# Attention and two expert layers on one core: the loads of the raw weights go from SyncE's queue to GpSimd's

## The chip, the core and the metric

The kernel runs on one core of one Trainium2 chip. The core has TensorE (PE in the rows, its weight loads PEld), VectorE (DVE), ScalarE (ACT), GpSimd (POOL) and SyncE (SP), and 16 DMA engines that every queue of the core feeds. The metric is the device time of one execution in microseconds, of which the median over some runs is given.

## The reference

```
kv  = einsum('bhsd,bhse->bhde', k, v)          # 8 batches, 8 heads, 576 tokens, 64 wide
out = einsum('bhsd,bhde->bhse', q, kv)
out = out / sqrt(mean(out * out, -1) + 1e-06) * g_norm
x   = out.transpose(0, 2, 1, 3).reshape(4608, 512)
h = x @ w_in1;  x = (h * clip(h + 3, 0, 6) / 6) @ w_out1      # 512 -> 2048 -> 512
h = x @ w_in2;  x = (h * cos(h)) @ w_out2
```

The four weight matrices arrive as 64-bit words, the rest as float32.

## The kernel before

The 4608 tokens are nine superblocks of 512. Each layer takes its 2048 inner features as eight pairs of 128-row blocks. A weight matrix comes in eight pieces of 1 MB (one pair each): `ri` is a piece of a w_in, `ro` of a w_out. The function `raw_load` (L208) loads a piece into one of three buffers with the tag `raw`; these buffers serve other tiles too. `decode` makes float32 of the 64-bit words: ScalarE at L245, VectorE at L247, L251 and L254, ScalarE again at L258 (a sum of squares), after which the raw buffer is free. The float32 piece is called `di` or `do`.

The program starts with attention for superblock 0: `kv_load` (L383, L388) and the loads of the last rows of k and v (`tail`, L933) bring k and v of the four pairs of heads of batch 0, `kv_pair` multiplies them on TensorE (L403), VectorE copies the result into `kvbd` (L412), `q_load` (L429) brings q, and `chunk` turns each 128 tokens of q into x: transpose (L435), copy on ScalarE (L446), product (L455), squares and copy on ScalarE (L459, L460), a short chain on VectorE (L465 to L475), transpose (L481), scale into `xr` (L487). Then superblock 0 goes through layer 1 in float32: `plain_1` (L1016, the product with `di`; L1022 and L1023 make `u` of it) and `plain_2` (L1031, the product with `do`), for 16 row blocks f, while the weights are also split into float16 halves. All later superblocks, and all of layer 2, run as Strassen-like products in float16 (L841, L660, L713).

All DMAs before the change are issued by SyncE, one after the other, in the order that a list scheduler gives the instructions of each engine when the program is built. An engine takes its instructions strictly in that order: one that waits holds all behind it.

Of the kernel before, what the change touches and what calls it, by code (L numbers as in the profile page):

```python
# [16 lines left out]
TOP = 2.0 ** 12  # L17
# [2 lines left out]
TWO_PI = 6.283185307179586  # L20
REBIAS = 2.0 ** -((1023 - 127) // 8)

# Winograd's form of Strassen's product, C = A B in 2x2 blocks:
#   S1 = A21+A22  S2 = S1-A11  S3 = A11-A21  S4 = A12-S2
#   T1 = B12-B11  T3 = B22-B12  T2 = T3+B11  N4 = B21-T2
# products in the order issued, with the accumulator each goes to:
PRODS = (
    ("A11", "B11", "P"),
    ("A12", "B21", "Q"),
# [26 lines left out]
def attention_moe_kernel(  # L56
# [12 lines left out]
    nc = tc.nc  # L69
    B, H, S, D = q.shape  # L70
# [4 lines left out]
    P = 128  # L75
# [39 lines left out]
    c3_t, gn, gs = (col() for _ in range(3))  # L115
    kvbd = const.tile([P, 2, NP, P], F32, name="kvbd")

    # ---- stages: each generator emits one stage per turn, so that consecutive
    # ---- stages, which wait on each other across engines, lie a turn apart
    active = []  # L120

    def start(gen):
# [22 lines left out]
        turn_of[0] += 1  # L145
        return ps_m.tile([P, 512], F32, tag=tag, name=name, bufs=2 if tag == "t" else 1)

    # ---- scales
    def pow2_scale(mx, name, squares, res, at=None):
        """[P, 1] magnitudes, or sums of squares that bound theirs -> res = (s, 1/s), s a power  # L150
        of two with s * max in [TOP, 2 TOP)."""
        pt = ps_scratch(f"pt_{name}")
        nc.tensor.transpose(out=pt[0:1, 0:P], in_=mx, identity=ident)
        m1 = col(p=1)
        nc.vector.tensor_reduce(
            out=m1, in_=pt[0:1, 0:P], axis=AX.X, op=ALU.max, apply_absolute_value=True
        )
        yield
        pb = ps_scratch(f"pb_{name}")
        nc.tensor.matmul(out=pb[:, 0:1], lhsT=ones_row, rhs=m1, start=True, stop=True)  # L160
        t = sm_p.tile([P, 1], F32, tag="sc", name=f"t_{name}")
        lo, hi = (2.0 ** -96, 2.0 ** 96) if squares else (2.0 ** -48, 2.0 ** 48)
        nc.vector.tensor_scalar(out=t, in0=pb[:, 0:1], scalar1=hi, scalar2=lo, op0=ALU.min, op1=ALU.max)
        pw = sm_p.tile([P, 1], U32, tag="pw", name=f"pw_{name}")
        if squares:
            nc.vector.tensor_scalar(
                out=pw, in0=t.bitcast(U32), scalar1=1, scalar2=0x3F800000,
                op0=ALU.logical_shift_right, op1=ALU.bitwise_and,
            )
        else:  # L170
            nc.vector.tensor_scalar(
                out=pw, in0=t.bitcast(U32), scalar1=0x7F800000, scalar2=None, op0=ALU.bitwise_and
            )
        s, inv = at or (col(), col())
        nc.vector.tensor_scalar(out=inv, in0=pw.bitcast(F32), scalar1=(2.0 ** 63 if squares else 1.0) / TOP, scalar2=None, op0=ALU.mult)
        nc.vector.reciprocal(out=s, in_=inv)
        res[name] = (s, inv)
        yield
# [12 lines left out]
    fac = [col(NG) for _ in range(2)]  # L191
    least = {}
    u0, b0, c0 = (col(NG) for _ in range(3))
    scale = {}
    scaled = set()
    sc1 = {}
    sc2 = {}

    # ---- weights: float64 words -> float32 -> scaled f16 hi and lo
    def raw_load(layer, kind, i):  # L200
        r = raw_p.tile([P, 1024, 2], U32, tag="raw", name=f"r{kind}{layer}_{i}")
        if kind == "i":
            src = w_ins[layer][:, 4 * i * P:4 * (i + 1) * P].rearrange("(k p) c -> p k c", p=P)
            dst = r.rearrange("p (k f) two -> p k (f two)", k=KD)
        else:
            src = w_outs[layer][2 * i * P:2 * (i + 1) * P, :].rearrange("(a p) c -> p a c", p=P)
            dst = r.rearrange("p (a e) two -> p a (e two)", a=2)
        nc.sync.dma_start(out=dst, in_=src)  # L208
        return r

    def group_scale(layer, kind, gi):
        """The scale of the weights of pairs 2 gi and 2 gi + 1."""
        mx = col()
        nc.vector.tensor_reduce(out=mx, in_=m_w[kind, layer][:, 2 * gi:2 * gi + 2], axis=AX.X, op=ALU.max)
        yield
        s, inv = s_w[kind, layer]
        yield from pow2_scale(
            mx, f"{kind}{layer}_{gi}", True, scale, (s[:, gi:gi + 1], inv[:, gi:gi + 1])
        )
        scaled.add((kind, layer, gi))  # L220

    def group_factors(layer):
        """fac = what brings each group's products to the scale common to all."""
        ts, tt = nc.vector.tensor_scalar, nc.vector.tensor_tensor
        fs = []
        for kind in "io":
            s, inv = s_w[kind, layer]
            m, f = col(), col(NG)
            nc.vector.tensor_reduce(out=m, in_=inv, axis=AX.X, op=ALU.max)
            yield  # L230
            ts(out=f, in0=s, scalar1=m, scalar2=None, op0=ALU.mult)
            yield
            nc.vector.reciprocal(out=f, in_=f)
            least[kind, layer] = m
            fs.append(f)
        yield
        tt(out=fac[layer], in0=fs[0], in1=fs[1], op=ALU.mult)
        yield

    def decode(r, t, sq):  # L240
        """float64 words r -> float32 t; sq = the sum of their squares. The upper half of a
        float64, taken for a float32, has the upper bits of the exponent for its exponent: a
        factor brings the bias to float32's, and what lies below its range to nothing."""
        hi, lo, tu = r[:, :, 1], r[:, :, 0], t.bitcast(U32)
        nc.scalar.activation(out=t, in_=hi.bitcast(F32), func=AF.Abs, scale=REBIAS)  # L245
        yield
        nc.vector.tensor_scalar(  # L247
            out=tu, in0=tu, scalar1=3, scalar2=0x7FFFFFFF, op0=ALU.logical_shift_left, op1=ALU.bitwise_and
        )
        yield  # L250
        nc.vector.scalar_tensor_tensor(  # L251
            out=tu, in0=hi, scalar=0x80000000, in1=tu, op0=ALU.bitwise_and, op1=ALU.bitwise_or
        )
        nc.vector.scalar_tensor_tensor(  # L254
            out=tu, in0=lo, scalar=29, in1=tu, op0=ALU.logical_shift_right, op1=ALU.bitwise_or
        )
        yield
        nc.scalar.activation(out=r[:, 0:512].bitcast(F32), in_=t, func=AF.Square, accum_out=sq)  # L258
        yield
# [25 lines left out]
        wf[kind, layer, i] = d  # L285

    def halves_i(layer, i):
        """The scaled f16 halves of the seven left operands of pair i."""
        key = f"i{layer}"
        dv = wf["i", layer, i].rearrange("p (k f) -> p k f", k=KD)  # L290
        a11, a12 = dv[:, 0:2, 0:P], dv[:, 2:4, 0:P]
# [35 lines left out]
            yield  # L327

    def halves_o1(i):
        """The scaled f16 halves of the seven right operands of pair i, layer 2."""  # L330
        d = wf["o", 1, i]
        dv = d.rearrange("p (a e) -> p a e", a=2)
        hd = DM // 2
# [41 lines left out]
        nc.sync.dma_start(out=w, in_=wi_dram[i])  # L375
        wts[f"i1_{i}"] = w

    # ---- attention: k v of one pair of heads, then chunks of 128 tokens of all heads
    def kv_load(b, p, t=None, tail=True):
        if t is None:  # L380
            t = kv_p.tile([P, 2, 2, 5, D], F32, tag="kv", name=f"kv{b}_{p}")
# [31 lines left out]
        yield  # L413

    def parts(c):
        """(batch, first row in it, first row in chunk c, rows) of the pieces of chunk c."""
        r, res = 0, []
        while r < P:
            b, s = divmod(c * P + r, S)
            n = min(P - r, S - s)  # L420
            res.append((b, s, r, n))
            r += n
        return res
# [66 lines left out]
            )  # L490
        yield

    # ---- a superblock's moving operands of the first product
    xraw = {}
    xops = {}

# [5 lines left out]
        yield  # L502

    def x_ops(layer, j):
        """Two stages per operand, in the order of the products."""
        while (layer, j) not in xraw:
            yield
        r = xraw.pop((layer, j))
# [34 lines left out]
            xops[layer, j] = ops  # L543
        free["raw"] += 1

    # ---- elementwise between the two products, on two pairs of row blocks at once
    gts = {}
    ready = []

    def relu6_part(j, gi, c, row, half):  # L550
        """c: [P, 2 pairs, 256] of row block `row` and token half `half`."""
        stt = nc.vector.scalar_tensor_tensor
        u = u_p.tile([P, 2, 256], F32, tag="u", name=f"u{j}_{gi}_{row}{half}")
        nc.scalar.activation(out=u, in_=c, func=AF.Relu, scale=u0[:, gi:gi + 1], bias=b0[:, gi:gi + 1])  # L554
# [57 lines left out]
        gop[j, nm, gi] = t  # L612

    def cos_operands(j, gi):
        """The halves of the seven left operands of the second product."""
        busy[0] += 1
        u = {}

# [63 lines left out]
        if e == 3:  # L682
            yield from x2_scales(j)

    # ---- second product of layer 2
    wo_s = {}
    n_wo = [0]
    bank2 = {}
# [2 lines left out]
    C_AT = {1: (0, 0), 4: (1, 1), 5: (0, 1), 6: (1, 0)}  # L691

    def wo_load():
        """The right operand of the next product."""
        j, n = divmod(n_wo[0], 7)
        if j == NSB:
            return
# [52 lines left out]
        )  # L750

    def units2(j):
        """The second product's pieces of superblock j, in order."""
        res = []
        late = []
        for n in range(7):
# [60 lines left out]
        now[0] += 1.0 / len(PRODS)  # L817

    def group(layer, j, gi, hooks):
        """The first product for pairs 2 gi and 2 gi + 1 over superblock j."""  # L820
        nm = f"{layer}_{j}_{gi}"
        ps, sn = {}, {}
        if layer == 1:
# [49 lines left out]
                turn()  # L873
                pop_mm2(1.0)

    # -- prologue
    scratch[:] = ["t", "acc0", "acc1", "acc2", "t", "acc3", "P", "R"]
    nc.vector.memset(c3_t, 3.0)
    nc.scalar.activation(out=col(), in_=c3_t, func=AF.Abs_reciprocal_sqrt)
# [99 lines left out]
    x_done = {}  # L979

    def attention():
        """The rest of the attention, chunk by chunk, into the superblocks' x."""
        n_kv, n_task = NP, 0
        kv_t[kvs[n_kv]] = kv_load(*kvs[n_kv])
        for c in (4, 5):
# [21 lines left out]
            n_task += 1  # L1007

    def plain_1(f):
        """Row block f of the first product in float32."""  # L1010
        w = wf["i", 0, f // 2].rearrange("p (k f) -> p k f", k=KD)
        ph = ps_m.tile([P, TT], F32, tag="PR"[f % 2], name=f"h0_{f}")
        step = P if f < SPLIT else TT
# [122 lines left out]
```

## Time and profile before

| | |
|---|---|
| runs | 1573.76, 1574.88, 1577.53 us (median 1574.88) |
| span of the profiled execution | 1573.6 us |
| TensorE busy | 1546.6 us, 98% |
| VectorE busy | 1227.5 us, 78% |
| ScalarE busy | 1052.4 us, 67% |
| DMA issues of raw weights | 16 of `ri`, 16 of `ro`, 1024 KB each |

The span runs from the first to the last instruction of the profiled execution. It lies 0.2 us below the fastest run and 1.3 us below the median, so what lies around the span is within the spread of the runs. TensorE idles for 27.0 us of the span. Times "at" a point are counted from the start of the span.

### The profile page before, as it was taken

The page shows a single profiled execution, that of the slowest core. Times are in us where ns is not written, and L with a number is a line of the kernel's source. Part 1 is how long each engine was busy: PE and PEld are TensorE (multiplying, and loading weights), DVE is VectorE, ACT ScalarE, POOL GpSimd, SP SyncE. Part 2 cuts the span into 40 slices and gives each one's busy share as a digit, 9 for nine tenths or more (in the row PEclk, how much of TensorE's full clock was granted, in tenths as well). Part 3 has the DMA queues.
Part 4 walks back from the last instruction along what each step waited for, and adds up shares of the span by engine and source line. Part 5 has one row for each costly group of instructions (what it writes and reads, how often), then busy time and mean ns, then how long its engine had stood idle before and what let it go on. Part 6 is the DMA issues. An engine that isn't in the chain of part 4 may idle for free.

```text
span 1573.6 us, 28793 instructions
## 1 busy us (share of the span) xinstructions
PE 1546.6 (98%) x11902; PEld 1179.6 (75%) x11902; DVE 1227.5 (78%) x2234; ACT 1052.4 (67%) x1714; POOL 0.7 (0%) x6
## 2 busy tenths in 40 slices
PE   7999999999999999999999999999999999999998
PEld 6444676676766766676666778888888888888887
DVE  4789876776768676967475799989898989889881
ACT  4566665665656564666355788878788888888771
POOL 0000000000000000000000000000000000000000
PEclk9999999999999999999999999999999999999999
DMA  6643422425151433312013142433334334243434
GB/s 181 220 147 109 121 94 81 135 64 171 42 167 51 129 113 100 117 34 81 21 35 114 48 154 101 141 115 128 116 127 148 127 115 155 92 151 121 143 110 157
DMA packets 112066, 180.11 MB, mean 114 GB/s; under 512 B 51008, under 2 KB 83776, under 8 KB 102720
## 3 DMA queue, kind: packets, MB, share of 16 engines
q1 hardware_dynamic: 111936, 178.28, 34.6%
q8 instruction: 93, 1.52, 0.4%
q14 instruction: 37, 0.30, 0.1%
HBM read 144.70 MB, written 33.55 MB: 113 GB/s over the span
## 4 chain that ended last, share of the span: by engine, by line
PE 55%; DVE 29%; ACT 11%; issue 2%; DMA 2%; SPq 0%; DVEq 0%
PE acc L660 20%; PE P L841 11%; DVE uA L593 5%; PE R L841 5%; DVE uA L598 5%; DVE gs_A L264 4%; PE kv L403 4%; DVE gs_S L264 4%; ACT uA L595 3%; PE h L1016 3%; PE acc L1031 3%; PE Q L841 3%; DVE c L857 2%; PE po L455 2%; ACT uA L596 2%
## 5 line engine op out<-in xcount | busy, mean ns | idle before, releaser
L841 PEld LDWEIGHTS <-wi 128*128 128x128 f16 x5712 | 557.4, 98 | 108.5 <-issue 4.9
L660 PE MATMUL acc<-g,wo 128*128 128x512 f16 x1536 | 368.6, 379 | 0.3 <-ACT g L567 0.3
L660 PEld LDWEIGHTS <-wo 128*128 128x128 f16 x1536 | 148.8, 98 | 134.7 <-issue 1.1
L841 PE MATMUL P<-xoB,wi 128*128 128x256 f16 x1536 | 190.3, 273 | 1.6 <-ACT sn L853 1.5
L841 PE MATMUL P<-xoT,wi 128*128 128x256 f16 x1536 | 189.1, 273 | 0.5 <-ACT sn L853 0.2
L713 PEld LDWEIGHTS <-gs_A 128*128 128x128 f16 x1632 | 159.7, 98 | 20.4 <-issue 1.9
L853 ACT ACTIVATE sn<-P 128x512 f32<-128x512 f32 x204 | 119.2, 584 | 70.0 <-PE P L841 69.4
L713 PEld LDWEIGHTS <-gs_S 128*128 128x128 f16 x1392 | 136.1, 98 | 22.3 <-issue 6.6
L595 ACT ACTIVATE uA<-uA,cols 128x512 f32<-128x512 f32 x144 | 103.6, 720 | 62.7 <-DVE uA L593 61.3
L554 ACT ACTIVATE u<-c,cols 128x512 f32<-128x512 f32 x96 | 77.9, 812 | 85.6 <-DVE c L857 66.2
L713 PE MATMUL P<-wo,gs_S 128*128 128x256 f16 x888 | 114.6, 273 | 5.3 <-ACT sn L732 5.3
L569 DVE TENSOR_TENSOR g<-u,g 128x512 f16<-128x512 f32 x128 | 87.6, 688 | 30.0 <-ACT g L567 29.1
L567 ACT ACTIVATE g<-u 128x512 f16<-128x512 f32 x128 | 80.1, 627 | 43.8 <-DVE u L556 43.4
L713 PE MATMUL P<-wo,gs_A 128*128 128x256 f16 x840 | 107.2, 273 | 1.6 <-ACT sn L732 1.6
L556 DVE SCALAR_TENSOR_TENSOR u<-u,cols,c 128x512 f32<-128x512 f32 x96 | 71.9, 749 | 38.1 <-ACT u L554 37.8
L262 ACT ACTIVATE gs_A<-uA,cols 128x512 f16<-128x512 f32 x125 | 88.3, 713 | 16.4 <-DVE uA L598 11.3
L264 DVE SCALAR_TENSOR_TENSOR gs_A<-uA,cols,gs_A 128x512 f16<-128x512 f32 x125 | 92.7, 747 | 7.4 <-ACT gs_A L262 5.4
L591 ACT ACTIVATE uA<-c,cols 128x512 int32<-128x512 f32 x108 | 77.2, 715 | 30.1 <-DVE c L862 21.9
L841 PE MATMUL R<-xoT,wi 128*128 128x256 f16 x768 | 94.7, 273 | 0.0
L841 PE MATMUL Q<-xoB,wi 128*128 128x256 f16 x768 | 94.6, 273 | 0.0
L841 PE MATMUL R<-xoN,wi 128*128 128x256 f16 x768 | 94.5, 273 | 0.0
L598 DVE SCALAR_TENSOR_TENSOR uA<-uA,c 128x512 f32<-128x512 f32 x108 | 74.1, 687 | 23.0 <-ACT uA L596 22.1
(203 smaller groups left out, 2298.4 us busy)
## 6 DMA issues: line engine op xcount, KB each, us to landing
wo<-wod SPq DMA_DIRECT2D x63, 1024.0 KB, 4.9
ri<-in_moe_w_in_dram SPq DMA_DIRECT2D x16, 1024.0 KB, 6.2
ro<-in_moe_w_out_dram SPq DMA_DIRECT2D x16, 1024.0 KB, 5.2
x2d<-o SPq DMA_DIRECT2D x36, 256.0 KB, 2.4
xr<-x2d SPq DMA_DIRECT2D x9, 1024.0 KB, 4.7
out_dram<-o SPq DMA_DIRECT2D x36, 256.0 KB, 3.8
q<-in_q_dram SPq DMA_DIRECT2D x30, 256.0 KB, 3.0
kv<-in_k_dram SPq DMA_DIRECT2D x29, 256.0 KB, 2.8
```

Of the source, the lines that this page charges most:

```text
L262: nc.scalar.activation(out=hi, in_=src, func=AF.Copy, scale=s)
L264: nc.vector.scalar_tensor_tensor(out=lo, in0=src, scalar=s, in1=hi, op0=ALU.mult, op1=ALU.subtract)
L554: nc.scalar.activation(out=u, in_=c, func=AF.Relu, scale=u0[:, gi:gi + 1], bias=b0[:, gi:gi + 1])
L567: nc.scalar.activation(out=gt[:, :, 0, sl], in_=u, func=AF.Copy)
L569: nc.vector.tensor_tensor(out=gt[:, :, 1, sl], in0=u, in1=gt[:, :, 0, sl], op=ALU.subtract)
L593: stt(out=u, in0=ui, scalar=nk, in1=c, op0=ALU.mult, op1=ALU.add)
L595: nc.scalar.activation(out=u, in_=u, func=AF.Sin, scale=hf)
L598: stt(out=u, in0=u, scalar=0.5 * SIG2, in1=c, op0=ALU.subtract, op1=ALU.mult)
L660: nc.tensor.matmul(out=acc[e], lhsT=w[:, a, row, e * P:(e + 1) * P], rhs=g[:, c], start=(n == 0 and i == 0), stop=(n == NF - 1 and i == 2),)
L713: nc.tensor.matmul(out=ps[:, mt], lhsT=g[:, c, pr, mt * P:(mt + 1) * P], rhs=w[:, i, a], start=(first and k == 0), stop=(end and k == 2), ...
L841: nc.tensor.matmul(out=ps[bank][:, pr], lhsT=w[:, a, A_AT[an], kk], rhs=x[:, c, kk], start=(first and pr == 0 and i == 0 and kk == 0), sto ...
L853: nc.scalar.activation(out=sn[n], in_=ps["P"], func=AF.Copy)
```

## The change

In `raw_load` the DMA is issued by GpSimd instead of SyncE:

```diff
             src = w_outs[layer][2 * i * P:2 * (i + 1) * P, :].rearrange("(a p) c -> p a c", p=P)
             dst = r.rearrange("p (a e) two -> p a (e two)", a=2)
-        nc.sync.dma_start(out=dst, in_=src)
+        nc.gpsimd.dma_start(out=dst, in_=src)
         return r
```

The other lines of the diff only blank comments. The list scheduler then orders the engines' instructions anew. The differences are all in the first part of the program, up to the last row blocks of superblock 0.

GpSimd's rows at the start of the program. `ident` is the identity that the transposes use; `ri_0` to `ro_1` are the first four raw pieces, of which the fourth has to wait for the first one's buffer:

```order
masks.py:197 MEMSET ident 128x128
+L208 DMA ri_0_150<-in_moe_w_in_dram 128x4x512
 masks.py:199 ISA
 masks.py:199 AFFINE_SELECT ident<-ident 128x128
+L208 DMA ro_0_361<-in_moe_w_out_dram 128x2x1024
+L208 DMA ri_1_397<-in_moe_w_in_dram 128x4x512
+L208 DMA ro_1_425<-in_moe_w_out_dram 128x2x1024
```

GpSimd had no DMA before; the third piece, `ri_1`, no longer follows a load of k and v.

SyncE's loads from the second batch's first pair of heads on, where `ri_1` stood behind the loads `kv_1` (k and v of the next pair):

```order
 L383 DMA kv_1_388<-in_v_dram 128x2x256
 L388 DMA kv_1_388<-in_v_dram 64x2x64
-L208 DMA ri_1_397<-in_moe_w_in_dram 128x4x512
-L208 DMA ro_1_425<-in_moe_w_out_dram 128x2x1024
-L208 DMA ri_2_530<-in_moe_w_in_dram 128x4x512
-L208 DMA ro_2_547<-in_moe_w_out_dram 128x2x1024
 L383 DMA kv_2_494<-in_k_dram 128x2x256
```

SyncE now goes from `kv_1` to `kv_2` with nothing between.

ScalarE's first rows. `di_0` is the first decoded piece, `pq` the transposed q, `tmp` its copy:

```order
+L245 ACTIVATE di_0_282<-ri_0_150 128x1024
+L258 ACTIVATE ri_0_150,cols<-di_0_282 128x1024
 L446 ACTIVATE tmp_222<-pq_224 128x512
 L446 ACTIVATE tmp_223<-pq_230 128x512
-L245 ACTIVATE di_0_282<-ri_0_150 128x1024
 L459 ACTIVATE tmp_222<-po_254 128x512
```

Both ScalarE steps of the first decode now stand ahead of all of the attention's.

VectorE's first rows, before and then changed (`kv_0` to `kv_3` are the products of the four pairs of heads):

```order
L412 COPY kvbd<-kv_0_157 64x64 x2
L412 COPY kvbd<-kv_1_170 64x64 x2
L412 COPY kvbd<-kv_2_183 64x64 x2
L412 COPY kvbd<-kv_3_196 64x64 x2
L247 TENSOR_SCALAR di_0_282<-di_0_282 128x1024
```

```order
L247 TENSOR_SCALAR di_0_282<-di_0_282 128x1024
L412 COPY kvbd<-kv_0_157 64x64 x2
L251 SCALAR_TENSOR_TENSOR di_0_282<-ri_0_150,di_0_282 128x1024
L254 SCALAR_TENSOR_TENSOR di_0_282<-ri_0_150,di_0_282 128x1024
L412 COPY kvbd<-kv_1_170 64x64 x2
```

The three VectorE steps of the first decode moved from among the steps of L465 to L475 to ahead of the copies of `kv_1` to `kv_3`; `di_1` moves likewise from behind `u_1` to ahead of it.

## Rows read from the trace of the kernel before

**Rows 1.** The page: span, and TensorE's and the other engines' busy time.

```profile
span 1573.6 us, 28793 instructions
PE 1546.6 (98%) x11902; PEld 1179.6 (75%) x11902; DVE 1227.5 (78%) x2234; ACT 1052.4 (67%) x1714; POOL 0.7 (0%) x6
```

**Rows 2.** Windows: stretch, length, busy PE, PEld, DVE, ACT, POOL; PEclk, DMA share, GB/s.

```profile
20.00:30.00 10.00, 5.85 (x44) 4.79 (x42) 8.43 (x30) 7.64 (x17) 0.00 (x0) 0.99 0.45 120
30.00:40.00 10.00, 9.89 (x75) 8.96 (x76) 6.05 (x16) 6.38 (x13) 0.00 (x0) 0.84 0.25 63
40.00:50.00 10.00, 8.56 (x37) 4.86 (x36) 4.11 (x5) 3.04 (x3) 0.00 (x0) 1.00 0.88 311
50.00:60.00 10.00, 9.62 (x41) 4.67 (x41) 9.23 (x21) 4.06 (x7) 0.00 (x0) 1.00 0.59 168
60.00:80.00 20.00, 20.00 (x65) 9.63 (x65) 17.02 (x29) 14.60 (x19) 0.00 (x0) 1.00 0.61 187
80.00:100.00 20.00, 20.00 (x82) 9.83 (x82) 16.83 (x35) 12.15 (x19) 0.00 (x0) 1.00 0.64 200
100.00:150.00 50.00, 49.97 (x162) 24.50 (x158) 46.19 (x93) 33.92 (x55) 0.00 (x0) 1.00 0.40 121
```

**Rows 3.** Waits in the first 60 us: total, times, longest (us); SPq is SyncE's queue.

```profile
PE kv L403 <- DMA kv<-in_v_dram: 4.4, 1, 4.4
...
PE px L481 <- DVE y L473: 2.6, 1, 2.6
...
PE h L1016 <- DVE di L254: 1.8, 1, 1.8
...
SPq L383 <- PE kv L403: 14.8, 2, 10.9
```

**Rows 4.** TensorE's waits from 60 us to the end, those for loads.

```profile
PE kv L403 <- DMA kv<-in_v_dram: 0.3, 2, 0.2
```

**Rows 5.** Timeline of the first 20 us: start, duration, engine, line, what.

```profile
3.85 0.47 SPq L383 DMA_DIRECT2D kvs<-in_v_dram  x1
...
8.35 2.47 SPq L208 DMA_DIRECT2D ri<-in_moe_w_in_dram  x1
8.65 0.93 PEld L403 LDWEIGHTS kv<-kvs 128*64 128x64 f32 x8
...
17.34 1.97 PE L435 MATMUL pq<-ident,q 128*128 128x128 f32 x8
...
18.49 0.60 ACT L446 ACTIVATE tmp<-pq 128x512 f32<-128x512 f32 x1 [16.26 <-PE pq L435]
```

**Rows 6.** DMA issues of the first 20 us: count, KB each, median us to landing.

```profile
ri<-in_moe_w_in_dram SPq DMA_DIRECT2D x1, 1024.0 KB, 7.6
...
kvs<-in_v_dram SPq DMA_DIRECT2D x3, 256.0 KB, 4.5
```

**Rows 7.** A window in which only raw pieces move (columns as in Rows 2).

```profile
44.00:46.00 2.00, 2.00 (x6) 0.94 (x5) 0.09 (x1) 0.15 (x1) 0.00 (x0) 1.00 1.02 395
```

**Rows 8.** Timeline: the first piece's decode among the attention's steps.

```profile
19.83 1.14 ACT L245 ACTIVATE di<-ri 128x1024 f32<-128x1024 f32 x1
...
21.00 0.69 DVE L247 TENSOR_SCALAR di<-di 128x1024 uint32<-128x1024 uint32 x1 [3.10 <-ACT di L245]
...
23.46 1.20 DVE L251 SCALAR_TENSOR_TENSOR di<-ri,di 128x1024 uint32<-128x1024 uint32 x1
...
25.06 1.21 DVE L254 SCALAR_TENSOR_TENSOR di<-ri,di 128x1024 uint32<-128x1024 uint32 x1
...
27.71 1.06 ACT L258 ACTIVATE ri<-di 128x1024 f32<-128x1024 f32 x1
```

**Rows 9.** Timeline: the issue of the second w_in piece.

```profile
38.27 0.60 SPq L208 DMA_DIRECT2D ri<-in_moe_w_in_dram  x1
```

**Rows 10.** DMA issues from 60 to 200 us, the raw pieces.

```profile
ri<-in_moe_w_in_dram SPq DMA_DIRECT2D x6, 1024.0 KB, 5.3
ro<-in_moe_w_out_dram SPq DMA_DIRECT2D x5, 1024.0 KB, 4.8
```

## The prediction

> **What bounds the kernel now.** I read the page first: TensorE is busy for 1546.6 of 1573.6 us, so it idles for 27.0 us in all, and nothing that only moves loads can give back more than that [rows 1]. Then I read its waits, to see how much of the idle time ends with a load. From 60 us on TensorE waits for loads for 0.3 us in all [rows 4]; none of these is a raw piece. So whatever the new queue does for the raw pieces that are issued after 60 us, most of the 32,, there is next to nothing to win there. What can move lies in the first 60 us. There the windows show TensorE idle for 4.15 us from 20 to 30 us, then 0.11, 1.44 and 0.38 us in the next three stretches, 6.1 us together [rows 2]. The waits name two large parts of it: 2.6 us before the transpose at L481, which waits for VectorE's short chain, and 1.8 us before the product at L1016, which waits for the decode of the second piece, `di_1` [rows 3]. A third wait, 4.4 us at the start, is for the very first k and v. From 60 to 150 us TensorE is full, and VectorE is the next engine: it has 3.0, 3.2 and 3.8 us left in the three stretches, 10.0 us of 90 [rows 2].
>
> All of this is under 0.5% of the time. A measurement of this kernel can tell about 0.3%, 4.7 us, from no change.
>
> **Gain 1: the first decode leaves VectorE's chain.** Before, `ri_0` is issued at 8.35 us and decoded while the attention's steps wait for VectorE: L247, L251 and L254 take 0.69, 1.20 and 1.21 us there [rows 5, 8]. In the new order they stand ahead of the copies of `kv_1` to `kv_3`, in a time in which VectorE mostly waits, since TensorE is still at the products of k and v (it sat idle for 3.10 us right before L247). That is 3.1 us off the stretch from 20 to 30 us, where VectorE is busy for 8.43 of 10 us and so sets the pace [rows 2]. Bounds: the two steps that lie directly between L466 and L473 are 2.4 us; all idle time of that stretch is 4.15 us. I take 3.1. ScalarE's two steps, 1.14 and 1.06 us, leave the same stretch [rows 8]; ScalarE has room there, so I count nothing for them.
>
> **Gain 2: the second piece no longer stands behind k and v.** `ri_1` was issued only at 38.27 us, because SyncE's next load in line waited up to 10.9 us for TensorE to finish with the buffer for k and v [rows 3, 9]. TensorE later waited 1.8 us for its decode. In the new order it is the third DMA of GpSimd and has to wait for nothing, and it is there long before 40 us. Gain 1.8 us, at most the 1.9 us that are idle from 30 to 60 us, at least nothing if the decode of `do_1`, which follows it, takes its place.
>
> **Cost: the raw pieces come ahead of k, v and q.** For a DMA issued by GpSimd the trace of before has no row. But three pieces, of which the first had been issued at 8.35 us and the third at 38.27 us [rows 5, 9], now start in the first microseconds, and the DMA engines are what the start waits for. Pieces of this kind alone move at 395 GB/s with the engines full (a share of 1.02) [rows 7]. Three of them are 3.15 MB, so 8.0 us of all sixteen engines. The load that TensorE needs next at that time is v of the second pair (`kvs`): issued at 3.85 us, landed 4.5 us later, at 8.35 us, and used at 8.65 us [rows 5, 6]. It has no slack. The three remaining pairs then keep TensorE busy until 17.34 us, 8.7 us [rows 5]. So what delays that load delays the transpose of q at L435 by as much, less 0.3 us.
>
> How long is the delay? Below, nothing: the raw pieces get only what SyncE's queue leaves free. Above, all three go ahead of it: 8.0 - 0.3 = 7.7 us. If the engines serve the two queues in equal parts, SyncE's loads up to that one, which took from about 2.5 us to 8.35 us (2.5 is an estimate: the first pair's 0.5 MB, 1.3 us at that rate, are there for TensorE at 4.4 us [rows 3], and their report takes some time too), take twice as long: 5.85 us more, less 0.3, and less about 0.3 for the time before the first raw bytes come, 5.2 us. I take 5.2, near the middle of the bounds. The later loads keep up in that case: they have the whole of the three pairs' 8.7 us.
>
> The Trainium skill ("DMA: Bandwidth & Descriptors", "Queues, rings and completion order") says that each DMA engine takes turns between the queues that have work, packet by packet. No row of this case has two data queues at work, so the trace can't yet confirm it; by that rule with its turns counted in packets rather than time, the 2 KB and 4 KB rows of the raw pieces would get more than half, and the delay would be nearer 7.7 than 5.2.
>
> **Does the first piece come in time?** ScalarE now has L245 and L258 of `di_0` ahead of L446, which it began at 18.49 us [rows 5]. The chain L245, L247, L251, L254, L258 needs 1.14 + 0.69 + 1.20 + 1.21 + 1.06 = 5.3 us [rows 8], so `ri_0` must land by 13.2 us, or by 18.4 us if TensorE is 5.2 us late. On SyncE's queue a piece took 7.6 us to land in a crowded stretch [rows 6]; from about 1 us, and with half of the engines, which adds its own 2.7 us, it lands at about 11.3 us. It comes in time, so the order itself costs nothing; if GpSimd were more than 7 us slower than that, this cover would be gone and every further microsecond would be lost.
>
> **Sum.** -3.1 - 1.8 + 5.2 = +0.3 us. The rest of the queue's work is counted at nothing: SyncE's loads of k, v and q after 60 us stand behind fewer others, but TensorE waited only 0.3 us for them [rows 4]; and layer 2's raw pieces come while TensorE is full. The halved clock in the stretch from 30 to 40 us (0.84 of full on the mean, so 1.6 us of work at full rate) follows the idle stretch from 20 to 30 us [rows 2]; whether it stays I can't tell, and I leave it as it is, as a gain of up to 1.6 us at the low end. The profiled span would be 1573.9 us; with the median 1.28 us above the span, I predict 1575.2 us.
>
> **Rivals.**
>
> *The raw pieces take only what is left* (chance 0.2). Then the cost goes and both gains stay: -3.1 - 1.8 = -4.9, with the clock up to -6.5. Time 1568.4 to 1570.0 us. For it: SyncE has its sixth load out at 3.85 us [rows 5], when GpSimd may not have its first bytes under way. Against it: the sixteen engines were full then.
>
> *All of the raw pieces go first* (0.15). +7.7 - 4.9 = +2.8, so 1577.7 us; with gain 1 at 2.4 and gain 2 at nothing it is +5.3, 1580.2 us. For it: their rows are 2 and 4 KB long, those of k and v 1 KB.
>
> *GpSimd and VectorE get in each other's way* (0.15; this is the case on the slower side). The mechanism: while GpSimd writes the work list of a load, a VectorE instruction of L247's kind waits, and VectorE falls behind in the stretch from 60 to 150 us. At most 11 raw pieces are issued there [rows 10], and VectorE has 10.0 us to spare [rows 2], so it decides from 0.9 us per piece on. If each piece holds VectorE for as long as SyncE took to issue `ri_0`, 2.47 us [rows 5], it is 11 x 2.47 - 10.0 = +17.2, time 1592.4 us; at 1.5 us each +6.5, time 1581.7 us. For it: VectorE is busy for 89% of the stretch. Against it: L247 is one short step per piece.
>
> The Trainium skill speaks against the change here ("SBUF — State Buffer", "Who interferes with whom"): VectorE's fast two-port mode and GpSimd share a port pair, and whichever comes first holds it, so loads issued by GpSimd can be starved by VectorE, or VectorE held. L247 runs 1024 elements in 0.69 us where L251 takes 1.20 us [rows 8], which agrees with L247 being in a faster mode; no row shows GpSimd at such work.
>
> *Nothing changes at all* (0.05): GpSimd is so slow to start that its pieces land as late as SyncE's did; both gains and the cost go, 1574.9 us.
>
> **How the numbers follow.** My forecast has 0.45, the rivals 0.2, 0.15, 0.15 and 0.05. The forecast's own range is 1572 to 1578 us. The range for 8 in 10 goes from 1569 us, within the first rival, to 1581 us, within the third, leaving out half of the first rival's better end and most of the third. Faster by over 0.3% (under 1570.2 us) is most of the first rival: 0.17. Slower by over 0.3% (above 1579.6 us) is most of the third, some of the second, and a late first piece: 0.19. The same: 0.64.
>
> **What would show it right or wrong.** Right: `kvs` lands later than 8.35 us and L435 starts at about 22 us instead of 17.34; L481's wait of 2.6 us and L1016's of 1.8 us are gone; TensorE is full from 60 us on as before, at the same point of the program within 1 us. Wrong: L435 starts as early as before (first rival); ScalarE waits at its first L245 for the load beyond 18 us; VectorE's L247 lasts or waits longer while GpSimd has a row; or TensorE waits for loads after 60 us.

## The result, and the profile after

The changed kernel takes 1587.32 us (median of 4 runs, 1586.43 to 1587.69). The kernel before took 1575.31 us on the same chip (4 runs, 1573.76 to 1577.53). The ratio is 1.0075, with a 95% interval of 1.0061 to 1.009: the change makes the kernel slower by about 12 us. The prediction was 1575.2 us with a range of 1569 to 1581 us, so it was wrong, range included.

The profiled execution took 1587.24 us, and its span of 1585.5 us is 11.9 us longer than before [rows 1]. The page of the changed kernel, span and busy times:

```profile
span 1585.5 us, 28830 instructions
...
PE 1548.4 (98%) x11902; PEld 1181.2 (75%) x11902; DVE 1229.4 (78%) x2234; ACT 1054.0 (66%) x1714; POOL 24.3 (2%) x38
```

TensorE now idles for 1585.5 - 1548.4 = 37.1 us instead of 27.0; that is 10.1 of the 11.9 us, and the other 1.8 us are in its busy time. To find where, I followed three instructions of TensorE through both traces: the first transpose of q (L435, the end of k and v for superblock 0), the first float16 product (L841), and the first L660 behind it. The rows of the last two in the kernel before:

```profile
166.95 1.47 PE L841 MATMUL P<-xoB,wi 128*128 128x256 f16 x12
...
186.18 2.80 PE L660 MATMUL acc<-g,wo 128*128 128x512 f16 x12
```

The timeline of the changed kernel at three places (start, duration, engine, line, what; in brackets the idle time before it and its releaser):

```profile
1.29 0.89 POOL L208 DMA_DIRECT2D ri<-in_moe_w_in_dram  x1 [0.35 <-issue]
...
2.53 0.62 SPq L933 DMA_DIRECT2D tail<-in_v_dram  x1
3.22 0.77 POOL L208 DMA_DIRECT2D ri<-in_moe_w_in_dram  x1
...
9.41 1.12 ACT L245 ACTIVATE di<-ri 128x1024 f32<-128x1024 f32 x1 [7.18 <-DMA ri<-in_moe_w_in_dram]
...
16.06 0.44 PE L403 MATMUL kv<-tail 64*64 64x64 f32 x2 [10.63 <-DMA tail<-in_v_dram]
...
26.56 1.11 PE L435 MATMUL pq<-ident,q 128*128 128x128 f32 x4
...
172.03 1.47 PE L841 MATMUL P<-xoB,wi 128*128 128x256 f16 x12
...
176.62 0.76 POOL L208 DMA_DIRECT2D ri<-in_moe_w_in_dram  x1 [28.88 <-ACT ri L258]
...
176.97 0.60 SPq L388 DMA_DIRECT2D kv<-in_v_dram  x1
...
183.41 1.89 PE L403 MATMUL kv<-kv 64*64 64x64 f32 x12 [3.17 <-DMA kv<-in_v_dram]
...
196.59 2.79 PE L660 MATMUL acc<-g,wo 128*128 128x512 f16 x12
...
381.77 0.72 POOL L208 DMA_DIRECT2D ro<-in_moe_w_out_dram  x1 [8.32 <-DVE u L556]
...
390.23 0.69 ACT L673 ACTIVATE o<-acc,cols 128x512 f32<-128x512 f32 x1 [2.03 <-DMA x2d<-o]
...
390.97 0.81 PE L660 MATMUL acc<-g,wo 128*128 128x512 f16 x3 [1.46 <-ACT o L673]
```

**The start.** GpSimd issues three raw pieces between 1.3 and 4.0 us, as the prediction had it. But TensorE then waits 10.6 us for `tail`, the small load of the last rows of v, and L435 comes at 26.56 instead of 17.34 us [rows 5], 9.2 us late. At L841 the program is only 5.1 us late (172.03 - 166.95); 4.1 us have been won back in between. **The second place.** At 176.6 us GpSimd issues the first raw piece of layer 2 in the midst of SyncE's loads of k and v. TensorE waits 3.2 us for one of them, and the first L660 is 10.4 us late: 5.3 us more. **The third place.** At 382 us a `ro` goes out, and the stores of layer 1's output (`x2d`) hold ScalarE and then TensorE for 1.5 us. 5.1 + 5.3 + 1.5 = 11.9 us, the whole difference of the spans.

TensorE's waits of the changed kernel, in the first 60 us:

```profile
PE kv L403 <- DMA tail<-in_v_dram: 10.6, 1, 10.6
PE kv L403 <- DMA kv<-in_v_dram: 4.3, 1, 4.3
PE po L455 <- ACT qT L446: 1.2, 1, 1.2
PE h L1016 <- ACT xr L487: 1.1, 1, 1.1
PE po L455 <- ACT tmp L446: 0.7, 1, 0.7
```

and from 60 us on:

```profile
PE kv L403 <- DMA kv<-in_v_dram: 3.2, 1, 3.2
...
PE acc L660 <- ACT o L673: 1.5, 1, 1.5
```

The waits of 2.6 us at L481 and 1.8 us at L1016 [rows 3] are gone, as predicted. The wait for `tail` is not new: the kernel before has it too, at 6.83 us, with 1.3 us.

```profile
6.83 0.44 PE L403 MATMUL kv<-tail 64*64 64x64 f32 x2 [1.30 <-DMA tail<-in_v_dram]
```

It grew by 9.3 us, and L435 comes 9.2 us later. The loads after 60 us, which had cost 0.3 us [rows 4], cost 3.2; for the load of v that TensorE now waits 3.2 us for, it had waited 0.18 us before (at 174.62 us).

**What the DMA engines did.** The DMA view of the changed kernel from 8 to 12 us: packets, MB, share of the 16 engines, for GpSimd's queue (q0) and SyncE's (q1).

```profile
q0 software_dynamic: 376, 1.45, 93.6%
q1 hardware_dynamic: 392, 0.10, 11.2%
```

Sixteen engines have 64 us in these 4 us. GpSimd's packets took 0.936 x 64 / 376 = 0.159 us each and carry 3.9 KB; SyncE's took 0.112 x 64 / 392 = 0.018 us each and carry 0.26 KB, the 256-byte rows of `tail`. The two queues sent packets in like numbers, and so SyncE's queue had 11% of the engines. (The two stretches before are less even, 114 packets to 38 from 4 to 6 us and 155 to 291 from 6 to 8 us; why that is stays open. From 10 to 12 us it is 191 to 191.) `tail` has 0.26 MB in such rows, 1024 packets, more than the 816 in which q0 sends all three raw pieces. The same view from 2 to 16 us (each issue with its count, KB, median us to landing):

```profile
q0 software_dynamic: 816, 3.15, 63.7%
...
tail<-in_k_dram SPq DMA_DIRECT2D x1, 128.0 KB, 12.5
tail<-in_v_dram SPq DMA_DIRECT2D x1, 128.0 KB, 13.4
```

In the kernel before the same stretch shows 4.4 and 4.2 us for these two loads:

```profile
tail<-in_k_dram SPq DMA_DIRECT2D x1, 128.0 KB, 4.4
tail<-in_v_dram SPq DMA_DIRECT2D x1, 128.0 KB, 4.2
```

At the second place it is the same kind of load, v's rows of 256 bytes. From 176 to 184 us in the changed kernel:

```profile
x2d<-o SPq DMA_DIRECT2D x1, 256.0 KB, 7.0
...
kv<-in_v_dram SPq DMA_DIRECT2D x1, 32.0 KB, 6.3
```

Before, the same two (171 to 175 us) took 2.9 and 2.7 us:

```profile
x2d<-o SPq DMA_DIRECT2D x1, 256.0 KB, 2.9
...
kv<-in_v_dram SPq DMA_DIRECT2D x1, 32.0 KB, 2.7
```

The windows of the changed kernel (columns as in [rows 2]):

```profile
30.00:40.00 10.00, 7.63 (x54) 6.74 (x53) 7.09 (x31) 7.54 (x19) 0.00 (x0) 1.00 0.18 40
60.00:150.00 90.00, 89.97 (x295) 43.31 (x296) 76.78 (x148) 58.80 (x84) 7.35 (x10) 1.00 0.46 145
...
180.00:182.00 2.00, 0.24 (x5) 0.10 (x2) 0.46 (x1) 1.51 (x2) 0.00 (x0) 1.00 0.96 371
182.00:184.00 2.00, 0.59 (x4) 0.50 (x5) 0.00 (x0) 0.16 (x1) 0.00 (x0) 0.51 0.47 172
184.00:186.00 2.00, 2.00 (x14) 1.69 (x14) 0.60 (x4) 0.00 (x0) 0.00 (x0) 0.50 0.05 12
186.00:188.00 2.00, 2.00 (x11) 1.69 (x10) 2.00 (x8) 0.00 (x0) 0.00 (x0) 0.50 0.64 150
```

The rows from 180 us on show why a wait of 3.2 us costs 5.3. TensorE was busy for only 0.83 of the 4 us from 180 to 184, and from 182 us to at least 188 us its granted clock was 0.51 and 0.50, the lower of its two levels (1.2 of 2.4 GHz). The 4.0 us that it is busy from 184 to 188 us are 2.0 us of work at the full clock; 3.2 + 2.0 = 5.2 us.

The rival of GpSimd and VectorE can be read here as well. From 60 to 150 us TensorE is as full as before (89.97 of 90 us, by [rows 2] the same), so nothing is lost there; VectorE is busy for 76.8 us instead of 80.0. And L247, the step that should have suffered from GpSimd, has the same median (min/median/max ns; before, then changed):

```profile
L247 DVE TENSOR_SCALAR di<-di x16: 671/694/695, 21.0 to 626.6; 128x1024 uint32<-128x1024 uint32 x16
```

```profile
L247 DVE TENSOR_SCALAR di<-di x16: 683/694/934, 10.6 to 638.7; 128x1024 uint32<-128x1024 uint32 x16
```

### The profile page after: what moved, and what is told of

Its sections match the earlier page's. It is cut to its first block, busy times and chain, and to the rows that moved or that the text cites. A ratio compares the mean times of both kernels' runs of the same rounds, so it can differ in the third digit from the quotient of the medians.

```text
span 1585.5 us, 28830 instructions
## 1 busy us (share of the span) xinstructions
PE 1548.4 (98%) x11902; PEld 1181.2 (75%) x11902; DVE 1229.4 (78%) x2234; ACT 1054.0 (66%) x1714; POOL 24.3 (2%) x38
## 4 chain that ended last, share of the span: by engine, by line
PE 57%; DVE 28%; ACT 11%; DMA 2%; issue 2%; SPq 0%; ACTq 0%
PE acc L660 19%; PE P L841 11%; PE R L841 5%; DVE uA L593 5%; DVE uA L598 4%; DVE gs_A L264 4%; PE kv L403 4%; PE acc L1031 4%; PE h L1016 4%; DVE gs_S L264 3%; ACT uA L595 3%; PE Q L841 3%; PE po L455 2%; DVE c L857 2%; ACT uA L596 2%; PE P L713 2%
## 5 line engine op out<-in xcount | busy, mean ns | idle before, releaser
L841 PEld LDWEIGHTS <-wi 128*128 128x128 f16 x5712 | 557.9, 98 | 109.0 <-issue 4.9
L660 PE MATMUL acc<-g,wo 128*128 128x512 f16 x1536 | 368.9, 379 | 1.9 <-ACT o L673 1.5
L660 PEld LDWEIGHTS <-wo 128*128 128x128 f16 x1536 | 148.8, 98 | 136.6 <-issue 3.2
L841 PE MATMUL P<-xoB,wi 128*128 128x256 f16 x1536 | 190.3, 273 | 1.6 <-ACT sn L853 1.5
L841 PE MATMUL P<-xoT,wi 128*128 128x256 f16 x1536 | 190.2, 274 | 0.5 <-ACT sn L853 0.4
L262 ACT ACTIVATE gs_A<-uA,cols 128x512 f16<-128x512 f32 x125 | 88.3, 713 | 16.2 <-DVE uA L598 11.3
L841 PE MATMUL R<-xoT,wi 128*128 128x256 f16 x768 | 94.8, 273 | 0.0
L841 PE MATMUL Q<-xoB,wi 128*128 128x256 f16 x768 | 94.6, 273 | 0.0
L841 PE MATMUL R<-xoN,wi 128*128 128x256 f16 x768 | 94.5, 273 | 0.0
```

The lines of the kernel that those rows point to most:

```text
L262: nc.scalar.activation(out=hi, in_=src, func=AF.Copy, scale=s)
L660: nc.tensor.matmul(out=acc[e], lhsT=w[:, a, row, e * P:(e + 1) * P], rhs=g[:, c], start=(n == 0 and i == 0), stop=(n == NF - 1 and i == 2),)
L841: nc.tensor.matmul(out=ps[bank][:, pr], lhsT=w[:, a, A_AT[an], kk], rhs=x[:, c, kk], start=(first and pr == 0 and i == 0 and kk == 0), sto ...
```

## The experiments

Four theories stood at the start. **A**: the engines take turns between the two queues packet by packet, so that the long packets of the raw pieces starve the short ones of `tail` and v. **B**: the new order of VectorE's and ScalarE's instructions costs the time. **C**: GpSimd's work holds up VectorE. **D**: something of GpSimd's queue alone, which another second queue would not do. Each experiment edits the one line L208 of the changed kernel, unless its text or diff says more. This table has the results; the ratios are to the kernel before on the same chip, all times in us, and the points in the program are those of the section on the result. "Start" is L435, "to L660" the time from the first L841 to the first L660, and "rest" the time from there to the end of the span. The last five columns are of one profiled execution each. The span of the kernel before ranges from 1571.1 to 1578.3 us over its runs, so a difference of 1 us in them means something only where a wait of that size stands in the rows.

| kernel | median | ratio, 95% | span | start | first L841 | to L660 | rest |
|---|---|---|---|---|---|---|---|
| before | 1575.31 | 1 | 1573.6 | 17.34 | 166.95 | 19.23 | 1387.4 |
| changed | 1587.32 | 1.0075, 1.0061 to 1.009 | 1585.5 | 26.56 | 172.03 | 24.56 | 1388.9 |
| e1_first3_sync | 1582.4 | 1.0045, 1.0029 to 1.0062 | 1580.6 | 17.10 | 166.31 | 26.21 | 1388.1 |
| e2_first3_gpsimd | 1581.11 | 1.003, 1.0017 to 1.0043 | 1578.5 | 26.04 | 172.35 | 19.08 | 1387.1 |
| e3_layer1_gpsimd | 1580.26 | 1.0028, 1.0017 to 1.0038 | 1578.7 | 27.00 | 172.59 | 19.28 | 1386.8 |
| e4_tail_first | 1587.53 | 1.0072, 1.0057 to 1.0087 | 1586.3 | 26.74 | 172.55 | 24.52 | 1389.2 |
| e5_first3_scalar | 1582.89 | 1.0043, 1.0029 to 1.0057 | 1579.8 | 21.95 | 167.27 | 23.39 | 1389.1 |
| e6_gated | 1574.31 | 0.9992, 0.9983 to 1.0001 | 1574.4 | 17.05 | 168.73 | 18.88 | 1386.8 |
| e7_gated_third | 1572.62 | 0.9982, 0.9973 to 0.9991 | 1570.1 | 16.98 | 164.40 | 18.91 | 1386.8 |
| e8_swap | 1577.61 | 1.0008, 1.0000 to 1.0017 | 1575.0 | 24.02 | 168.54 | 19.17 | 1387.3 |
| e9_one_piece | 1577.81 | 1.0009, 1.0000 to 1.0019 | 1574.4 | 21.25 | 167.75 | 19.20 | 1387.4 |
| e10_sync_ahead | 1573.5 | 0.9985, 0.9976 to 0.9993 | 1570.9 | 17.02 | 164.24 | 18.80 | 1387.9 |

**e1: the first three pieces go back to SyncE.**

```diff
-        nc.gpsimd.dma_start(out=dst, in_=src)
+        (nc.gpsimd if (layer, kind, i) not in ((0, "i", 0), (0, "o", 0), (0, "i", 1)) else nc.sync).dma_start(out=dst, in_=src)
```

> The first three raw pieces (ri_0, ro_0, ri_1) go back to SyncE's queue, the other 29 stay on GpSimd's. Theory A (the DMA engines take turns between the two queues packet by packet, so GpSimd's 4 KB packets hold up SyncE's small ones): TensorE's transpose of q at L435 starts at 17 to 18 us again instead of 26.6, and the 5 us lost up to the first float16 product are back; the second loss, where a raw piece of layer 2 meets a load of k and v near 176 us, can stay: 1575 to 1582 us. Theory B (the new order of VectorE and ScalarE costs the time): the order is nearly that of before, so 1575 us. Theory C (GpSimd at work holds up VectorE): 29 of 32 pieces are still GpSimd's, so 1586 us.

The start is as before (L435 at 17.10 us), and so is the first L841 but for 0.6 us. The second place remains and is even larger, two waits for v instead of one:

```profile
174.86 0.65 PE L403 MATMUL kv<-kv 128*64 128x64 f32 x8 [1.07 <-DMA kv<-in_v_dram]
179.05 1.75 PE L403 MATMUL kv<-kv 64*64 64x64 f32 x12 [3.54 <-DMA kv<-in_v_dram]
```

So the loss at the start hangs on these three pieces, and the others cost 7.0 us of span by themselves.

**e2: only the first three pieces go to GpSimd.**

```diff
-        nc.gpsimd.dma_start(out=dst, in_=src)
+        (nc.gpsimd if (layer, kind, i) in ((0, "i", 0), (0, "o", 0), (0, "i", 1)) else nc.sync).dma_start(out=dst, in_=src)
```

> Only the first three raw pieces are issued by GpSimd, the other 29 by SyncE. Theory A: L435 near 26.6 us as in the changed kernel, the loss of about 5 us at the start is all there is, no wait of 3 us at L403 near 180 us: 1580 us. Theory B: most of the new order at the start is kept, 1580 to 1587 us. Theory C: three pieces at the start, when VectorE is idle, cost nothing: 1575 to 1576 us.

The reverse of e1: the wait for `tail` is there with 10.0 us, and TensorE waits neither for v at the second place nor at L673 at the third. e1 and e2 together add 7.0 + 4.9 = 11.9 us to the span, as much as the change itself, so no other large loss is hidden. That the sum is so exact is luck: place by place e1 and e2 have 5.4 (e2, at L841), 7.0 and 0.7 us (e1) where the change has 5.1, 5.3 and 1.5, and by the medians they add 7.2 + 5.9 = 13.1 us to 12.0.

**e3: only layer 1 goes to GpSimd.**

```diff
-        nc.gpsimd.dma_start(out=dst, in_=src)
+        (nc.gpsimd if layer == 0 else nc.sync).dma_start(out=dst, in_=src)
```

> All raw pieces of layer 1 stay with GpSimd, those of layer 2 go back to SyncE. TensorE, VectorE and ScalarE have exactly the order of the changed kernel. Theory A: the start stays as slow (L435 at 26.6 us), TensorE's wait of 3.2 us at L403 near 180 us and the half clock after it go: 5 to 7 us less than the changed kernel, 1580 to 1582 us. Theory B: the same order, the same time, 1587 us. Theory C: VectorE is short of time only in layer 1, so 1587 us.

The orders of TensorE, VectorE and ScalarE in the trace are here those of the changed kernel, instruction for instruction. The start is lost as there, but from L841 on the kernel runs like before (19.28 and 1386.8 us). So it is layer 2's pieces on GpSimd's queue that cost the second and third place, and the orders do not (theory B falls there); layer 1's other pieces cost nothing that shows.

**e4: `tail` is issued ahead of the first pair's k and v.**

```diff
-    kv_t[0, 0] = kv_load(0, 0, tail=False)
     for n, src in enumerate((k, v)):
         nc.sync.dma_start(out=tail[:, n], in_=src[0, :, 512:576, :].rearrange("h p d -> p h d"))
+    kv_t[0, 0] = kv_load(0, 0, tail=False)
```

> The changed kernel with the two tail loads (256-byte packets) issued ahead of the first k and v instead of behind them. Theory A, with turns counted in packets: the tail is through before GpSimd's first bytes come, its wait of 10.6 us goes, and 64 packets of 1 KB per engine up to the second pair's v stand against GpSimd's 48 of 4 KB: that pair starts at about 14 us and L435 at about 23 us instead of 26.6; 3 to 4 us less, 1583 to 1584 us. If the turns were equal in time, the order of the loads would change nothing: 1587 us. Theory B: the same order on VectorE and ScalarE, 1587 us.

The 1583 to 1584 us that I had given for theory A were missed: the time is that of the change. The wait moved. Only the first half of `tail` got through before the raw pieces came (its k landed 2.7 us after issue, its v 7.3), and now the first pair's own k and v starved: TensorE waits 15.2 us for them. The DMA view from 8 to 12 us, when those loads, whose rows are 1 KB long, share the engines with the raw pieces:

```profile
q0 software_dynamic: 328, 1.28, 79.8%
q1 hardware_dynamic: 345, 0.32, 23.5%
```

Packet for packet, 328 to 345, and the engines 80 to 24. This is A's mechanism at its plainest, and it shows what A's number had overlooked: any load that comes behind the raw pieces' start pays, not `tail` alone.

**e5: the first three pieces go to ScalarE's queue.**

```diff
-        nc.gpsimd.dma_start(out=dst, in_=src)
+        (nc.scalar if (layer, kind, i) in ((0, "i", 0), (0, "o", 0), (0, "i", 1)) else nc.gpsimd).dma_start(out=dst, in_=src)
```

> The first three raw pieces are issued by ScalarE's queue instead of GpSimd's, the other 29 stay with GpSimd; the order of TensorE is that of the changed kernel. Theory A (turns packet by packet, whatever queue): ri's packets are 2 KB on a queue like SyncE's (84 ns instead of 159), so the tail's 64 packets per engine wait for less: the tail lands at about 12.5 us instead of 16.1, L435 starts 3 to 4 us earlier than 26.6 us, 1583 to 1585 us. Theory D (something of GpSimd's queue alone, such as a higher rank in the DMA engines): no starving, L435 near 19 us, 1580 us or less.

ScalarE's queue (q10) is another hardware queue, like SyncE's. Its packets hold 2.6 KB (2.10 MB in 800), and SyncE's loads starve beside it too. The DMA view from 2 to 12 us, and TensorE's first wait for v:

```profile
q10 hardware_dynamic: 800, 2.10, 54.1%
q1 hardware_dynamic: 2275, 1.45, 49.8%
```

```profile
9.30 1.08 PE L403 MATMUL kv<-kv 128*64 128x64 f32 x8 [9.30 <-DMA kv<-in_v_dram]
```

From 6 to 8 us the two queues sent 178 and 177 packets, with 81% and 25% of the engines. The start comes 4.6 us late and 4.6 us earlier than in the changed kernel, where A gave 3 to 4, and the load that TensorE waits for is the first pair's v, not `tail`. But here the third piece went out only at 11.34 us, behind the first L245 in ScalarE's order, and two pieces are less than three. D falls: a second queue starves the first without GpSimd.

**e6: layer 1 stays on GpSimd, but the first piece has to wait for q; layer 2 goes back to SyncE.** A copy of one element of q into the raw buffer, made by GpSimd, holds GpSimd's queue until the second of the four loads of q has landed; the load then writes over it.

```diff
+        if (layer, kind, i) == (0, "i", 0): nc.gpsimd.tensor_copy(out=r[0:1, 0:1, 0], in_=q_t[1][0:1, 0, 0:1].bitcast(U32))
-        nc.gpsimd.dma_start(out=dst, in_=src)
+        (nc.gpsimd if layer == 0 else nc.sync).dma_start(out=dst, in_=src)
```

> Layer 1's raw pieces on GpSimd, but the first one waits (through a one-element copy into its buffer) until the second load of q has landed; layer 2's pieces on SyncE. Theory A: the start is as fast as before (L435 at 17 to 18 us), no wait at L403 near 180 us, TensorE's wait of 1.8 us for di_1 gone: 1573 to 1575 us, at most 1 us late because the third and fourth loads of q meet the raw pieces. Theory B: 1575 us.

The loss at the start is gone, with the same pieces on GpSimd's queue: there it is the overlap that costs, not the queue. (The second and third losses are gone as in e3, because layer 2's pieces are SyncE's.) But no gain is clear of the noise either: the first piece is decoded only from 29.48 us, TensorE waits 1.5 us at L1016 for it, which A had as gone, and 2.1 us at L481, and its clock was lower in that stretch (0.60 of full from 30 to 40 us, 0.84 before [rows 2]). This low clock is not part of every execution: the profiled one took 1576.19 us with a mean granted clock of 0.997, and six of the eleven took 1572.76 to 1574.31 us with 0.999 or 1.000. The pieces, now behind the start, share the engines with the later loads of q, of which two took 11.2 us to land.

**e7: the first two pieces stay on SyncE as before, and the others of layer 1 go to GpSimd, from the third on, which waits for the last q of the start.**

```diff
+        if (layer, kind, i) == (0, "i", 1): nc.gpsimd.tensor_copy(out=r[0:1, 0:1, 0], in_=qs[0:1, 1, 0, 0:1].bitcast(U32))
-        nc.gpsimd.dma_start(out=dst, in_=src)
+        (nc.gpsimd if layer == 0 and (kind, i) not in (("i", 0), ("o", 0)) else nc.sync).dma_start(out=dst, in_=src)
```

> As e6, but ri_0 and ro_0 stay on SyncE as before, and GpSimd's first piece, ri_1, waits until the fourth load of q has landed. Theory A: the start is that of before to the microsecond (L435 at 17.3 us), ri_1 is there before TensorE asks for di_1: the wait of 1.8 us goes and nothing comes in its place, 1573 to 1574 us. Theory B: the order of VectorE changes a little, 1575 to 1577 us.

Faster than the kernel before, by 0.18%. `ri_1` goes out at 19.78 instead of 38.27 us [rows 9], the wait at L1016 is gone, the one at L481 stays at 2.6 us. L841 comes 2.6 us earlier than before.

**e8: the queues change places: the raw pieces stay on SyncE, and the start's loads of k, v and q (but not g) go to GpSimd.** `kv_load` and `q_load` got a parameter for the engine, which only the calls of the start set. The diff, cut to three of the edited calls, is against the kernel before:

```diff
-    kv_t[0, 0] = kv_load(0, 0, tail=False)
+    kv_t[0, 0] = kv_load(0, 0, tail=False, eng=nc.gpsimd)
...
-        nc.sync.dma_start(out=tail[:, n], in_=src[0, :, 512:576, :].rearrange("h p d -> p h d"))
+        nc.gpsimd.dma_start(out=tail[:, n], in_=src[0, :, 512:576, :].rearrange("h p d -> p h d"))
...
-        q_t[c] = q_load(c)
+        q_t[c] = q_load(c, eng=nc.gpsimd)
```

> The other way round: all raw pieces on SyncE as before, but the start's k, v, tail and four loads of q on GpSimd. Theory A says that what is served in small packets loses. If GpSimd's queue packs the short rows of k, v and q into packets of 4 KB, its loads win two thirds of the engines against ri's 2 KB: L435 at 18 to 19 us, ri_0 decoded ahead, 1571 to 1575 us. If its packets are as short as the rows, the start starves as in the changed kernel, L435 at 24 us or later, 1580 us or more.

The time that A gave was missed here. SyncE had its first raw piece out at 0.74 us, and the raw pieces had the engines while GpSimd issued k and v one by one, 0.7 us each, so TensorE's first wait is 11.2 us and L435 comes at 24.02 us. By its time the run tells less than it was meant to, but two things can be read from it. GpSimd's queue moved these loads, whose rows are 256 bytes and 1 KB, in 1056 packets of 3.2 KB on the mean (the DMA view of the whole span):

```profile
q0 software_dynamic: 1056, 3.41, 0.6%
```

And once both queues had work, the longer packets won, as A says, although they were now those of k, v and q (the view from 12 to 16 us):

```profile
q0 software_dynamic: 290, 0.95, 62.0%
q1 hardware_dynamic: 289, 0.60, 40.2%
```

The numbers of packets are nearly equal, and the queue with the longer ones, 3.3 KB to 2.1 KB, has the larger share; A had given it two thirds.

**e9: only the very first piece goes to GpSimd.**

```diff
-        nc.gpsimd.dma_start(out=dst, in_=src)
+        (nc.gpsimd if (layer, kind, i) == (0, "i", 0) else nc.sync).dma_start(out=dst, in_=src)
```

> Only ri_0 is issued by GpSimd, all other raw pieces by SyncE. Theory A as a dose: GpSimd has 16 packets of 4 KB per engine instead of 48, so after 16 turns, 2.5 us of the engines, SyncE's loads have them alone. The tail's wait falls from 10.6 to about 3.5 us and L435 starts at 19.5 to 20 us, 2.5 us late instead of 9.2; the decode of ri_0 is still ahead of the attention, which gives up to 3 us back: 1574 to 1577 us. Theory B (the order alone): ScalarE and VectorE still have L245 to L258 of ri_0 first, so most of the loss at the start, 4 to 5 us, stays: 1579 to 1580 us.

The dose: one piece makes TensorE wait 5.3 us for `tail` and L435 3.9 us late, where three make it 10.6 and 9.2.

```profile
10.75 0.44 PE L403 MATMUL kv<-tail 64*64 64x64 f32 x2 [5.32 <-DMA tail<-in_v_dram]
```

A's direction holds, its sizes do not: it gave a wait of 3.5 us and L435 2.5 us late. ScalarE and VectorE begin in the order of the changed kernel, so the order alone, theory B, doesn't make the start 9.2 us late. 3.1 of the 3.9 us are won back by L841, where the first decode no longer stands among the attention's steps; the sum is 0.8 us, in the span too, and the ratio, 1.0009, doesn't tell it from nothing.

**e10: all pieces on SyncE, with `ri_1` ordered right behind `ro_0`.**

```diff
-        nc.gpsimd.dma_start(out=dst, in_=src)
+        with tc.high_priority(4000 if (layer, kind, i) == (0, "i", 1) else 0): nc.sync.dma_start(out=dst, in_=src)
```

> The kernel before, all loads on SyncE, but ri_1 is issued right behind ro_0 instead of behind the k and v that wait for TensorE. If all that GpSimd's queue gained in e7 is that ri_1 no longer stands behind that wait, this gains the same without GpSimd: TensorE's wait of 1.8 us for di_1 gone, 1572.5 to 1574 us. If e7's gain comes from a second queue beside SyncE's, this stays at 1575 us.

`ri_1` goes out at 16.35 us, the wait at L1016 is gone, L841 comes 2.7 us earlier than before, and the gain is that of e7 (0.9985 and 0.9982, within each other's intervals) without GpSimd. What e7 won came from the place of one load in the order, with what the scheduler moves on the other engines for it, and not from the queue.

**What follows.** A stands for the first two places: the losses come and go with the overlap of raw pieces with short-packet loads (e1, e2, e3, and e6 at the start), grow with the number of pieces (e9), move to whichever load is behind them (e4), don't need GpSimd (e5), and the two queues send like numbers of packets in most stretches (e4, e5, e8). A's times were missed clearly in e4 and e8, where it named the wrong load or the wrong start, and by about 1 us or less in e1, e2, e5, e7 and e9; in e9 it had the wait too short, and in e6 a wait as gone that stayed. B falls at the second and third place by e3, and at the start by e9. C was not tried by itself; L247's times speak against it, and e6 and e7, in which GpSimd issues most of layer 1, show no loss. At the third place the queue is shown to matter (e3 has no wait of TensorE there, e1 1.3 us), but that packets do it is only argued from the loads of k and v there, which took 4.9 to 5.6 us to land.

## Why the prediction was wrong, by its own steps

**What bounds the kernel.** Right that raw pieces after 60 us have next to nothing to win. The step that failed was to take this for "counted at nothing": that TensorE waits only 0.3 us for later loads [rows 4] doesn't say that they have time to spare. The load of v that cost 3.2 us is one of the two that it had waited for, so it came just in time. "Layer 2's raw pieces come while TensorE is full" is true, and it is how they starve what TensorE needs next. This term was 0; it measured 5.3 + 1.5 = 6.8 us, over half of the loss.

**Cost at the start.** The direction was right, the size was not: 5.2 predicted, 9.2 measured at L435, above even the upper bound of 7.7. The step that failed is "If the engines serve the two queues in equal parts". They served them in equal numbers of packets, with 94% of the engines' time to 11% from 8 to 12 us. The Trainium skill says that an engine takes turns between queues packet by packet ("DMA: Bandwidth & Descriptors", "Queues, rings and completion order"); the prediction set this beside its sum for want of a row, and the rows now agree, with packets as the trace counts them (328 to 345 in the same 4 us of e4, 290 to 289 in e8). The bound failed by its choice of load. It looked at v of the second pair (`kvs`) and gave it no slack, with 4.5 us to landing; that is the median of three, and the view from 2 to 4 us has 3.9 us for this one, so it was there at about 7.75 us, 0.9 us ahead of its use. The load without slack was `tail`: TensorE already waited 1.3 us for it before the change. Its v landed 13.4 instead of 4.2 us after its issue, 9.2 us later, while GpSimd's packets held the engines for 63.7% of the 14 us from 2 to 16 us, 8.9 us, and not the 8.0 of the bound. "The later loads keep up" was wrong in the same way.

**Gain 1 and gain 2.** Both waits went, as predicted. 4.1 us were won between L435 and L841, against 4.9 predicted, but not as written. The windows between these two points, before and then changed (columns as in [rows 2]):

```profile
17.34:166.95 149.61, 143.35 (x561) 77.91 (x560) 124.45 (x274) 96.17 (x151) 0.00 (x0) 0.99 0.48 147
```

```profile
26.56:172.03 145.47, 142.38 (x561) 77.79 (x561) 123.03 (x271) 95.17 (x148) 9.59 (x13) 1.00 0.42 130
```

TensorE idled for 6.26 us before and for 3.09 us after, 3.2 us less, and it was busy for 1.0 us less. Waits for ScalarE (1.2, 0.7 and 1.1 us, where there had been 0.9 us in all) took part of L481's place. The 1.0 us fits the clock: it stays at its full level from 30 to 40 us, where it had been 0.84 on the mean, a gain that the prediction put at up to 1.6 us and left aside. Gain 2 alone can be read from e7 and e10, where L481's wait and the lower clock stay: from L435 to L841 they take 147.4 and 147.2 us instead of 149.6, a gain of 2.2 to 2.4 us for 1.8 predicted.

**Does the first piece come in time?** Yes: ScalarE began L245 at 9.41 us, where I had 11.3; the piece was needed by 13.2.

**The sum by these terms.** Predicted: -4.9 + 5.2 + 0 = +0.3. Measured: -4.1 + 9.2 + 6.8 = +11.9 us.

**The rivals.** "All of the raw pieces go first" (0.15) had the mechanism nearest to the truth, and its +2.8 to +5.3 us hold the 5.1 us at L841; it too had nothing for what comes later. "GpSimd and VectorE get in each other's way" gives a time in the right region (1581.7 to 1592.4 us) for a reason that the trace doesn't bear out. The rule of the Trainium skill beside it ("SBUF — State Buffer", "Who interferes with whom"), by which GpSimd's loads and VectorE's fast mode hold each other up, left no mark of that size: L247's median is 694 ns before and after, the longest of 16 grew from 695 to 934 ns, and GpSimd took 0.71 to 0.89 us for an issue at the start. "The raw pieces take only what is left" is the reverse of what happened at the start.

## What to carry to other kernels

A second queue is no second road: the DMA engines are shared, and where packets take turns a queue of long packets takes most of them. Before a bulk load gets its own queue, list the loads that run at the same time with the length of their rows, and look for the one with the most packets whose landing an engine waits for; a load that is waited for 0.3 us is one without slack. If a bulk load is late because it stands behind a waiting load, move it in the order of its own queue first: here that gave 0.15%, where the queue of its own cost 0.75%.

## What the runs showed of the hardware that was not expected

For all rows tried here, GpSimd's queue sent packets of 3 to 4 KB on the mean: 3.9 KB for the raw pieces (3.15 MB in 816), 3.2 KB for loads with rows of 256 bytes and 1 KB (e8). ScalarE's hardware queue sent the first pieces in packets of 2.6 KB (e5). In most stretches in which two queues had work they sent packets in nearly equal numbers, whichever of them had the long ones (376 to 392 after the change, 328 to 345 in e4, 178 to 177 in e5, 290 to 289 in e8). And with a wait of 3.2 us in the midst of full work TensorE's granted clock fell to half, and stayed there for 4 us and more of the work behind the wait, which added 2.0 us to its price.
